# An FFN of selected tokens, computed for two batches at once by seven block products

## The chip, the cores and the metric

The kernel runs on one core of one Trainium2 chip. The metric is device time in microseconds of one execution; the median of three runs is given. The profile is one execution recorded by the hardware profiler; its span is a little shorter than the run's time.

Words for the engines: TensorE (PE) does matrix products, with PEld its loads of the stationary operand; VectorE (DVE) and ScalarE (ACT) do elementwise work and reductions, GpSimd (POOL) elementwise work in SBUF and gathers; SyncE (SP) issues transfers. PSUM is the memory that TensorE writes to.

## The reference

Attention with pooled queries feeds a mixture of depths: of each batch's 576 tokens the 128 with the highest gate score go through an FFN (512 to 1024 to 512 with a relu), the rest pass unchanged. Everything is fp32.

```
# q, k, v: (8 batches, 8 heads, 1152, 64); capacity 128
q_pool = q.reshape(B, H, S // 2, 2, D).mean(axis=3)
attn   = softmax(q_pool @ k.T / sqrt(D));  x = (attn @ v) as (B, 576, 512)
scores = einsum('bsd,d->bs', x, w_gate)
for b in range(B):
    top_idx = np.argpartition(-scores[b], capacity)[:capacity]
    xe = x[b, top_idx]                       # 128 x 512
    h  = np.maximum(xe @ w1, 0.0)            # w1: 512 x 1024
    ye = h @ w2                              # w2: 1024 x 512
    g  = 1.0 / (1.0 + np.exp(-scores[b, top_idx]))
    out[b, top_idx] = x[b, top_idx] + g[:, None] * ye
```

## The kernel before

The work is cut into 64 half-steps: 8 batches, 4 pairs of heads, 2 halves of the queries. In each, TensorE first makes the scores of this half, ScalarE takes their exponents, and TensorE then multiplies the exponents of the half before with the values.

```
        qs = slice(half["s"] * n, (half["s"] + 1) * n)
        p = half["p"] = self.work.tile([P, self.NG, G, 2, n], F32, name="p")
        for c in range(self.NC):
            sc = self.banks()
            for e in range(2):
                keys = slice(e * self.D, (e + 1) * self.D)
                for j in range(2):
                    rows = slice(j * self.D, (j + 1) * self.D)
                    nc.tensor.matmul(
                        sc[keys, j, 0:n],
                        lhsT=pair["kT"][rows, c * P + keys.start : c * P + keys.stop],
                        rhs=pair["qT"][rows, qs],
                        start=True,
                        stop=True,
                    )
            nc.scalar.activation(p[:, c // G, c % G, :, :], sc[:, :, 0:n], AF.Exp, scale=self.scale)

    # ... [cut] weighted(): the same loop with v, into one tile of two banks, then

        two = self.small.tile([P, 2, n], F32, name="two", bufs=2)
        nc.scalar.copy(two[:, :, :], av[:, :, 0:n])
        half["av"] = self.small.tile([P, n], F32, name="av", bufs=2)
        nc.gpsimd.tensor_tensor(
            out=half["av"][:, :], in0=two[:, 0, :], in1=two[:, 1, :], op=ALU.add
        )

    # ... [cut] folded(): the sums of exponents
        for u in range(G):
            nc.gpsimd.tensor_tensor(
                out=acc[:, u, :], in0=units[:, 0, u, :], in1=units[:, 1, u, :], op=ALU.add
            )
        fold = self.small.tile([P, 2, G * nb], F32, name="fold")
        for a, of in enumerate((units[:, 2, :, :], acc[:, :, :])):
            nc.vector.tensor_reduce(
                fold[:, a, :],
                of.rearrange("p u (m d) -> p (u m) d", d=BLK),
                AX.X,
                ALU.add,
                apply_transpose=True,
            )
```

For a pair to come, VectorE transposes keys and queries (`prepare_pair`: `kT`, L735, and `qT`) in even half-steps. Products with the gate weights and their sums:

```
        # multiplied():
        self.nc.gpsimd.tensor_tensor(
            out=pair["prod"][:, ns, :],
            in0=pair["avb"][:, ns, :],
            in1=self.w_gate[:, hp : hp + 1, :].broadcast_to([P, hb, BLK]),
            op=ALU.mult,
        )
        # ... [cut] gated():
        nc.vector.tensor_reduce(pair["red"][:, ns], pair["prod"][:, ns, :], AX.X, ALU.add)
        if half["s"] == 1:
            nc.vector.tensor_tensor(
                out=pair["part"][:, pair["hp"], :],
                in0=pair["red"][:, :],
                in1=pair["rec"][:, :],
                op=ALU.mult,
            )
```

A batch's tokens are ranked by VectorE (`routed`), their rows are gathered from the output in DRAM, transposed, put through both layers, added and scattered back. `yield` cuts this into pieces that the main loop takes between the attention products; a yield of `"mid"` or `"hidden"` says where. Here from the gather on:

```
            nc.gpsimd.indirect_dma_start(
                out=xe[0:w, :],
                out_offset=None,
                in_=rows_out,
                in_offset=bass.IndirectOffsetOnAxis(ap=index[0:w, 0:1], axis=0),
                bounds_check=(b + 1) * Sp - 1,
                oob_is_err=False,
            )

            xeT = ffn.tile([P, self.ND, P], F32, name="xeT")
            pv = self.banks()[:, 0, :].rearrange("p (c n) -> p c n", n=P)
            for c in range(self.ND):
                nc.tensor.transpose(
                    pv[:, c, 0:w], xe[0:w, c * P : (c + 1) * P], self.ident[0:w, 0:w]
                )
            nc.scalar.copy(xeT[:, :, 0:w], pv[:, 0 : self.ND, 0:w])
            yield mid

            hT = ffn.tile([P, self.NFC, P], F32, name="hT")
            for f0 in range(0, self.NFC, 4):
                pv = self.banks()[:, 0, :].rearrange("p (c n) -> p c n", n=P)
                for f in range(4):
                    for c in range(self.ND):
                        nc.tensor.matmul(
                            pv[:, f, 0:w],
                            lhsT=self.w1[:, c, (f0 + f) * P : (f0 + f + 1) * P],
                            rhs=xeT[:, c, 0:w],
                            start=(c == 0),
                            stop=(c == self.ND - 1),
                        )
                    if f == 3:
                        nc.scalar.activation(hT[:, f0 : f0 + 4, 0:w], pv[:, :, 0:w], AF.Relu)
                    yield "hidden" if f0 + f == self.NFC - 1 else False

            ps = self.banks()[:, 0, :]
            for f in range(self.NFC):
                nc.tensor.matmul(
                    ps[0:w, 0 : self.Dm],
                    lhsT=hT[:, f, 0:w],
                    rhs=self.w2[:, f, :],
                    start=(f == 0),
                    stop=(f == self.NFC - 1),
                )
                yield False
            if b == self.B - 1:
                nc.vector.scalar_tensor_tensor(
                    out=xe[0:w, :],
                    in0=ps[0:w, 0 : self.Dm],
                    scalar=own_gate[0:w, 0:1],
                    in1=xe[0:w, :],
                    op0=ALU.mult,
                    op1=ALU.add,
                )
            else:
                y = ffn.tile([P, self.Dm], F32, name="y", bufs=1)
                nc.scalar.activation(
                    y[0:w, :], ps[0:w, 0 : self.Dm], AF.Copy, scale=own_gate[0:w, 0:1]
                )
                if b < self.B - 2:
                    yield True
                nc.gpsimd.tensor_tensor(out=xe[0:w, :], in0=y[0:w, :], in1=xe[0:w, :], op=ALU.add)
            # ... [cut] scattered back by an indirect transfer
```

The main loop of half-steps, its body cut to the order of the work:

```
        for h in range(n_halves + 1):
            # ... [cut] even half-steps take the next pair; odd ones load another
                    pair["part"] = part
                else:
                    loaded = None
                    if n + 2 < len(pairs):
                        loaded = self.load_pair(*pairs[n + 2])
                        self.load_values(loaded)
                    if n > 1:
                        self.stored(halves[h - 4]["pair"])
                # ... [cut]
                self.scores(half)
                if h > 1:

                    of = halves[h - 2 - s]["pair"]
                    if s == 0:
                        of["groups"] = self.side_by_side(of["sum"].rearrange("p j n -> p (j n)"))
                    else:
                        self.spread(of)
                self.units(mid=True)
                if h > 2:
                    self.gated(halves[h - 3])
                self.folded(half)
                if h > 1:
                    self.multiplied(halves[h - 2])
                if s == 0 and loaded:
                    upcoming = loaded
                    self.prepare_pair(upcoming)
            # ... [cut] the last step, weighted(), drained(), normalized(), units(mid=False)
```

After the loop the remaining pieces of the last three batches are put in an order by hand: `older` (batch 5), `old` (batch 6), `new` (batch 7). Batch 7's scores are brought into a row by a matmul with a diagonal (L1054) and ranked from there.

```
        pieces(older, self.NFC - 2)
        pieces(new, 1)
        pieces(older, 2)
        pieces(new, 3)
        pieces(older)
        pieces(old, self.NFC)
        pieces(new, 1)
        low = self.counted()
        pieces(old, self.NFC - 3)
        pieces(new, 2)
        pieces(old)
        count = self.outside(low)
        pieces(new)
```

Of the kernel before, what the change touches and what calls it, by code (L numbers as in the profile page):

```python
# [534 lines left out]
class _Plain:  # L535
# [10 lines left out]
    def __init__(self, ctx, tc, q, k, v, moe_w_gate, moe_w1, moe_w2, capacity, out):  # L546
# [27 lines left out]
        assert 0 < self.TAIL < P and self.Dm == self.ND * P and self.Dm <= 512  # L574
        assert self.F == self.NFC * P and self.NFC % 4 == 0
# [17 lines left out]
        self.w2 = self.const.tile([P, self.NFC, self.Dm], F32, name="w2")  # L593

# [21 lines left out]
    def constants(self):  # L616
# [13 lines left out]
        slot_i = self.ffn.tile([P, self.Sp], I32, name="cmp", bufs=1)  # L630
        nc.gpsimd.iota(slot_i[:, :], pattern=[[1, self.Sp]], base=0, channel_multiplier=0)
        self.slot_f = const.tile([P, self.Sp], F32, name="slot_f")
        nc.vector.tensor_copy(self.slot_f[:, :], slot_i[:, :])
# [34 lines left out]
    def line_of_scores(self):  # L668

        line = self.ffn.tile([P, self.NT * P], F32, name="sc_row")  # L670
        self.nc.gpsimd.memset(line[0:1, self.Sp :], 0.0)
        return line
# [24 lines left out]

    def load_pair(self, b, hp):  # L700
# [3 lines left out]
        qb = self.load.tile([P, self.QB, 2, BLK], F32, name="qb")  # L704
# [8 lines left out]
    def load_values(self, pair):  # L713
# [3 lines left out]
        v_sb = pair["v"] = self.load.tile([P, 2, self.NC, self.D], F32, name="v_sb", bufs=3)  # L717
# [23 lines left out]
    def load_first(self, b, hp):  # L741
# [3 lines left out]
        kb = self.load.tile([P, self.KB, BLK], F32, name="kb")  # L745
        kn = kb.rearrange("p n d -> p (n d)").rearrange("p (c j d) -> p c j d", c=NC, j=2)
        acc = self.work.tile([P, G, 2 * self.HALF], F32, name="acc")
        third = self.QB // 3
        qn = acc.rearrange("p u n -> p (u n)")[0 : 3 * BLK, 0 : 4 * third * D]
        qn = qn.rearrange("p (j m d) -> p j m d", j=2, d=D)  # L750
        v_sb = self.load.tile([P, 2, NC, D], F32, name="v_sb", bufs=3)
# [11 lines left out]
        return {"k": kn, "q": qn, "v": v_sb, "b": b, "hp": hp}  # L763

    def prepare_first(self, pair):
# [5 lines left out]
        acc = self.work.tile([P, G, 2 * self.HALF], F32, name="acc")  # L771
        qp = acc.rearrange("p u n -> p (u n)")[0:rows, 0 : 2 * third * D]
        qp = qp.rearrange("p (n j d) -> p n j d", j=2, d=D)
# [76 lines left out]
    def folded(self, half):  # L850
# [9 lines left out]
        fold = self.small.tile([P, 2, G * nb], F32, name="fold")  # L860
# [8 lines left out]
        if half["s"] == 0:  # L869
            pair["sum"] = self.small.tile([P, 2, self.QB], F32, name="sum")  # L870
# [126 lines left out]
    def routed(self, b, part):  # L997
# [13 lines left out]
        if b < self.B - 1:  # L1011
# [27 lines left out]
            if b < self.B - 2:  # L1039
                yield True  # L1040
# [431 lines left out]
```

## Time and profile before

| | |
|---|---|
| median of 3 runs | 708.19 us (706.77 to 708.98) |
| span of the profiled execution | 704.8 us |
| matmuls of scores, L818 | 295.2 us busy |
| matmuls with the values, L836 | 294.6 us busy |
| first FFN layer, L1208 | 59.3 us busy, 512 instructions |
| second FFN layer, L1221 | 57.3 us busy, 128 instructions |
| bytes moved by transfers | 82.86 MB, 118 GB/s on average |

Lines named L... are lines of the kernel. A matmul in fp32 is recorded as two instructions. Busy times of matmuls overlap, so the sum over the lines is more than the time that they take. A row of the profile's table of groups gives line, engine, operation, operands, count, then the busy time, the mean duration in ns, and the idle time of the engine before them. The chain of work that ended last is followed back from the last instruction: at each step to what released it. A row of the waits gives who waited for what: total us, how often, the longest.

### The profile page before, as it was taken

The page shows a single profiled execution, that of the slowest core. Times are in us where ns is not written, and L with a number is a line of the kernel's source. Part 1 is how long each engine was busy: PE and PEld are TensorE (multiplying, and loading weights), DVE is VectorE, ACT ScalarE, POOL GpSimd, SP SyncE. Part 2 cuts the span into 40 slices and gives each one's busy share as a digit, 9 for nine tenths or more (in the row PEclk, how much of TensorE's full clock was granted, in tenths as well). Part 3 has the DMA queues.
Part 4 walks back from the last instruction along what each step waited for, and adds up shares of the span by engine and source line. Part 5 has one row for each costly group of instructions (what it writes and reads, how often), then busy time and mean ns, then how long its engine had stood idle before and what let it go on. Part 6 is the DMA issues. An engine that isn't in the chain of part 4 may idle for free.

```text
span 704.8 us, 23397 instructions
## 1 busy us (share of the span) xinstructions
PE 694.4 (99%) x9948; PEld 516.8 (73%) x9948; DVE 496.5 (70%) x793; ACT 444.5 (63%) x963; POOL 485.1 (69%) x452
## 2 busy tenths in 40 slices
PE   8999999999999999999999999999999999999996
PEld 5668899996758866688656887578775787766573
DVE  3877777996559965498754988559774697689540
ACT  6677778777547775477746776467754777477210
POOL 5877777868658695586955779467874877686520
PEclk9999999999999999999999999999999999999999
DMA  8888887858486483756928468382775728432200
GB/s 175 172 178 180 171 166 137 146 116 161 85 149 111 85 162 75 145 97 111 172 40 159 81 129 160 66 148 61 161 130 85 135 56 169 83 72 62 45 31 35
DMA packets 389490, 82.86 MB, mean 118 GB/s; under 512 B 376640, under 2 KB 376640, under 8 KB 389376
## 3 DMA queue, kind: packets, MB, share of 16 engines
q1 hardware_dynamic: 387872, 76.49, 58.1%
q0 software_dynamic: 1280, 4.20, 1.8%
q8 instruction: 80, 1.31, 0.8%
q10 hardware_dynamic: 224, 0.59, 0.3%
q14 instruction: 34, 0.28, 0.1%
HBM read 69.65 MB, written 11.59 MB: 115 GB/s over the span
## 4 chain that ended last, share of the span: by engine, by line
PE 89%; POOL 5%; issue 2%; DMA 1%; ACT 1%; DVE 1%; SPq 0%; POOLq 0%; DVEq 0%; ACTq 0%
PE ps L836 36%; PE ps L818 36%; PE ps L1208 8%; PE ps L1221 7%; POOL acc L857 2%; ACT p L825 1%; DMA kb<-in_k_dram 1%; DMA xe<-out_dram,index 1%; PE ps L1197 1%; POOL prod L925 1%; POOL x L956 0%; POOL av L846 0%; DVE fold L862 0%; POOL index L1175 0%; SPq L759 0%
## 5 line engine op out<-in xcount | busy, mean ns | idle before, releaser
L825 ACT ACTIVATE p<-ps 128x576 f32<-128x576 f32 x576 | 320.2, 695 | 1.7 <-PE ps L818 1.3
L818 PE MATMUL ps<-qT,kT 64*64 64x288 f32 x4608 | 295.2, 404 | 0.2 <-ACT p L825 0.2
L836 PE MATMUL ps<-p,v_sb 64*64 64x288 f32 x4608 | 294.6, 403 | 0.0
L857 POOL TENSOR_TENSOR acc<-p 128x576 f32<-128x576 f32 x192 | 266.3, 1417 | 15.4 <-ACT p L825 15.1
L836 PEld LDWEIGHTS ps<-p,v_sb 64*64 64x64 f32 x4608 | 215.5, 133 | 65.3 <-ACT p L825 9.2
L818 PEld LDWEIGHTS ps<-qT,kT 64*64 64x64 f32 x4608 | 208.0, 132 | 73.0 <-ACT p L825 15.4
L862 DVE TRANSPOSE_TENSOR_REDUCE fold<-p 128x54 f32<-128x1728 f32 x64 | 126.0, 1969 | 50.2 <-ACT p L825 50.2
L862 DVE TRANSPOSE_TENSOR_REDUCE fold<-acc 128x54 f32<-128x1728 f32 x64 | 125.3, 1957 | 46.0 <-POOL acc L857 45.8
L844 ACT COPY two<-ps 128x576 f32<-128x576 f32 x64 | 40.9, 639 | 156.9 <-PE ps L836 143.8
L846 POOL TENSOR_TENSOR av<-two 128x288 f32<-128x288 f32 x64 | 51.2, 800 | 96.5 <-ACT two L844 94.9
L915 DVE STREAM_TRANSPOSE avb<-av 128x288 f32<-128x288 f32 x64 | 29.4, 460 | 66.5 <-POOL av L846 66.5
L956 POOL TENSOR_TENSOR x<-avb,rec 128x576 f32<-128x576 f32 x32 | 37.1, 1159 | 40.3 <-DVE rec L954 27.9
L1208 PEld LDWEIGHTS ps<-xeT,w 128*128 128x128 f32 x512 | 57.8, 192 | 2.7 <-ACT p L825 2.6
L1208 PE MATMUL ps<-xeT,w 128*128 128x128 f32 x512 | 59.3, 277 | 0.0
L1221 PE MATMUL ps<-w,hT 128*128 128x512 f32 x128 | 57.3, 598 | 0.0
L925 POOL TENSOR_TENSOR prod<-avb,w_gate 128x288 f32<-128x288 f32 x64 | 51.5, 805 | 0.6 <-DVE avb L915 0.6
L902 ACT ACTIVATE sums<-total,tiny 32x18 f32<-32x18 f32 x124 | 38.1, 308 | 15.9 <-DVE total L893 14.2
L732 POOL TENSOR_TENSOR qp<-qb 128x576 f32<-128x576 f32 x31 | 43.8, 1414 | 2.2 <-DMA qb<-in_q_dram 2.2
L1221 PEld LDWEIGHTS ps<-w,hT 128*128 128x128 f32 x128 | 23.6, 190 | 28.1 <-issue 25.8
L735 DVE STREAM_TRANSPOSE kT<-kb 128x1152 f32<-128x1152 f32 x31 | 42.5, 1370 | 0.0
L887 ACT COPY groups<-sum 32x36 f32<-32x36 f32 x124 | 27.1, 219 | 6.7 <-DVE sum L872 5.2
L981 DVE TENSOR_TENSOR part<-red,rec 128x18 f32<-128x18 f32 x32 | 27.0, 845 | 1.1
(95 smaller groups left out, 290.6 us busy)
## 6 DMA issues: line engine op xcount, KB each, us to landing
kb<-in_k_dram SPq DMA_DIRECT2D x124, 144.0 KB
qb<-in_q_dram SPq DMA_DIRECT2D x124, 144.0 KB
v_sb<-in_v_dram SPq DMA_DIRECT2D x124, 144.0 KB
out_dram<-x SPq DMA_DIRECT2D x128, 72.0 KB
lines<-row_rank SPq DMA_DIRECT2D x7, 640.0 KB
w<-in_moe_w_dram SPq DMA_DIRECT2D x8, 512.0 KB
sc_row<-row SPq DMA_DIRECT2D x7, 288.0 KB
acc<-in_q_dram ACTq DMA_DIRECT2D x2, 288.0 KB
```

The costliest lines, as they stand in the source:

```text
L732: nc.gpsimd.tensor_tensor(out=qp[:, :, :], in0=pair["q"][:, :, 0, :], in1=pair["q"][:, :, 1, :], op=ALU.add)
L735: nc.vector.transpose(kT.rearrange("p (c g i) -> p c g i", c=self.NC, i=BLK), pair["k"].rearrange("p (g c) d -> p c g d", c=self.NC),)
L818: nc.tensor.matmul(sc[keys, j, 0:n], lhsT=pair["kT"][rows, c * P + keys.start : c * P + keys.stop], rhs=pair["qT"][rows, qs], start=True, ...
L825: nc.scalar.activation(p[:, c // G, c % G, :, :], sc[:, :, 0:n], AF.Exp, scale=self.scale)
L836: nc.tensor.matmul(av[j * self.D : (j + 1) * self.D, e, 0:n], lhsT=half["pair"]["v"][keys, j, c, :], rhs=half["p"][keys, c // G, c % G, j, :],
L844: nc.scalar.copy(two[:, :, :], av[:, :, 0:n])
L846: nc.gpsimd.tensor_tensor(out=half["av"][:, :], in0=two[:, 0, :], in1=two[:, 1, :], op=ALU.add)
L857: nc.gpsimd.tensor_tensor(out=acc[:, u, :], in0=units[:, 0, u, :], in1=units[:, 1, u, :], op=ALU.add)
L862: nc.vector.tensor_reduce(fold[:, a, :], of.rearrange("p u (m d) -> p (u m) d", d=BLK), AX.X, ALU.add, apply_transpose=True,)
L925: self.nc.gpsimd.tensor_tensor(out=pair["prod"][:, ns, :], in0=pair["avb"][:, ns, :], in1=self.w_gate[:, hp : hp + 1, :].broadcast_to([P, ...
L1208: nc.tensor.matmul(pv[:, f, 0:w], lhsT=self.w1[:, c, (f0 + f) * P : (f0 + f + 1) * P], rhs=xeT[:, c, 0:w], start=(c == 0), stop=(c == self ...
L1221: nc.tensor.matmul(ps[0:w, 0 : self.Dm], lhsT=hT[:, f, 0:w], rhs=self.w2[:, f, :], start=(f == 0), stop=(f == self.NFC - 1),)
```

## The change

For two batches the FFN's products are 2 x 2 block products: the tokens of two batches, each cut in two along the inner dimension, times the weights cut in quarters. Such a product needs eight block products done directly; with sums of the blocks taken beforehand seven are enough. The change does this for batches 0 to 5, in three pairs; batches 6 and 7 keep the direct layers. For it

- VectorE makes four sums of quarters of each layer's weights once, in sixteen pieces, one in each of the half-steps 11 to 26 (counted from 0); they are kept in DRAM and loaded back for each layer in turn into one tile `tw`;
- GpSimd makes four sums of the activations for each layer (`input_sums`);
- ScalarE copies each block product out of PSUM, and VectorE adds them in place (`seven_products`);
- ScalarE applies the relu to both batches' hidden values from SBUF, in one half-step; `scale` by the gate is then a step of its own.

To make room in SBUF several buffers are shared or fewer (query buffer 1 of 2, values 2 of 3, `prod` 1 of 2). The values are loaded one pair later. The product `part` goes from VectorE to GpSimd except at the end, `index` from GpSimd to VectorE, the division `x` to the following half-step. The order after the loop is new. TensorE's order of a pair is now: 56 matmuls of layer 1 in one half-step, three half-steps later 28 matmuls of layer 2; for the pair of batches 4 and 5 layer 2 stands after the last attention product.

```diff
+    def weight_sums(self):
+
+        nc = self.nc
+        for layer in (2, 1):
+            b11, b12, b21, b22 = (self.quarter(layer, i, j) for i in range(2) for j in range(2))
+            t1, t2, t3, t4 = (self.summed(layer, i) for i in range(4))
+            kept = self.tw_kept[layer] = self.dram.tile(
+                [P, 4, self.tw.shape[-1]], F32, name=f"tw{layer}", bufs=1
+            )
+            for i, (to, x, y) in enumerate(((t1, b12, b11), (t2, b22, t1), (t3, b22, b12), (t4, b21, t2))):
+                n = to.shape[1] // 2
+                for c in (slice(0, n), slice(n, 2 * n)):
+                    nc.vector.tensor_tensor(
+                        out=to[:, c, :], in0=x[:, c, :], in1=y[:, c, :], op=ALU.subtract
+                    )
+                    if c.start:
+                        nc.sync.dma_start(kept[:, i, :], self.tw[:, i, :])
+                    yield
+
+    def load_sums(self, layer):
+        for i in range(0, 4, 2):
+            self.nc.sync.dma_start(self.tw[:, i : i + 2, :], self.tw_kept[layer][:, i : i + 2, :])
+            yield
+
 
 
 # ... [cut] load_pair(): qb with bufs=1; load_values(): v_sb with bufs=2; multiplied(): prod with bufs=1
+            ending = pair["b"] == self.B - 1 and pair["hp"] >= self.NPAIR - 2
+            engine = nc.vector if ending else nc.gpsimd
+            engine.tensor_tensor(
                 out=pair["part"][:, pair["hp"], :],
                 in0=pair["red"][:, :],
                 in1=pair["rec"][:, :],
                 op=ALU.mult,
             )
 # ... [cut] routed(): after the transposes of the gathered rows
+            token = {"xe": xe, "xeT": xeT, "gate": own_gate, "index": index, "rows": rows_out, "w": w, "b": b}
+            if b >= self.paired:
+                yield mid
+                yield from self.layers(token)
+            elif b % 2 == 0:
+                self.first_of_two = token
 # ... [cut] else layers_of_two(); layers(): the two layers as before
+    def input_sums(self, a, s):
+
+        a11, a12, a21, a22 = a
+        s1, s2, s3, s4 = s
+        add, subtract = ALU.add, ALU.subtract
+        for i, (to, x, y, op) in enumerate(
+            ((s1, a21, a22, add), (s2, s1, a11, subtract), (s3, a11, a21, subtract), (s4, a12, s2, subtract))
+        ):
+            self.nc.gpsimd.tensor_tensor(out=to, in0=x, in1=y, op=op)
+            if i % 2:
+                yield i == 3
+
+    def seven_products(self, layer, a, s, c, rest, shape):
+
+
+
+        nc = self.nc
+        (a11, a12, _, a22), (s1, s2, s3, s4), (c11, c12, c21, c22) = a, s, c
+        b11, b21, b22 = (self.quarter(layer, i, j) for i, j in ((0, 0), (1, 0), (1, 1)))
+        t1, t2, t3, t4 = (self.summed(layer, i) for i in range(4))
+        u, x, y = rest
+
+        steps = (
+            (a11, b11, c11, ()),
+            (s1, t1, c22, ()),
+            (s3, t3, c21, ()),
+            (s2, t2, u, ((u, c11), (c21, u), (u, c22), (c22, c21))),
+            (s4, b22, c12, ((c12, u),)),
+            (a12, b21, x, ((c11, x),)),
+            (a22, t4, y, ((c21, y),)),
+        )
+        copies = []
+        for i, (of, by, to, _) in enumerate(steps):
+            if i % 2 == 0:
+                tile = self.banks()
+            ps, n = shape(tile[:, i % 2, :]), of.shape[1]
+            for f in range(by.shape[2] // P if layer == 1 else 1):
+                for k in range(n):
+                    if layer == 1:
+                        args = ps[:, f, :], by[:, k, f * P : (f + 1) * P], of[:, k, :]
+                    else:
+                        args = ps, of[:, k, :], by[:, k, :]
+                    nc.tensor.matmul(
+                        args[0], lhsT=args[1], rhs=args[2], start=k == 0, stop=k == n - 1
+                    )
+
+            copies.append((to, ps))
+            last = i == len(steps) - 1
+            if i % 2 or last:
+                for copy in copies:
+                    nc.scalar.copy(*copy)
+                copies = []
+            yield "sums" if last else False
+        for *_, sums in steps:
+            for to, of in sums:
+                nc.vector.tensor_tensor(out=to, in0=to, in1=of, op=ALU.add)
+
+    def layers_of_two(self, tokens):
+
+        nc, ffn, w = self.nc, self.ffn, tokens[0]["w"]
+
+        def quarters(tiles, n):
+            return [tile[:, i * n : (i + 1) * n, 0:w] for tile in tiles for i in range(2)]
+
+        def lines(bank):
+            return bank.rearrange("p (f n) -> p f n", n=P)[:, :, 0:w]
+
+        yield True
+        a = quarters([token["xeT"] for token in tokens], self.ND // 2)
+        room, s = self.room_of_sums(self.ND // 2, w)
+        for _ in self.input_sums(a, s):
+            pass
+        yield "mid"
+        hidden = [ffn.tile([P, self.NFC, P], F32, name="hT") for _ in tokens]
+        c = quarters(hidden, self.NFC // 2)
+
+        rest = [lines(room[:, i]) for i in (2, 3, 0)]
+        yield from self.seven_products(1, a, s, c, rest, lines)
+        yield "mid"
+        for tile in hidden:
+            nc.scalar.activation(tile[:, :, 0:w], tile[:, :, 0:w], AF.Relu)
+        loads = self.load_sums(2)
+        next(loads)
+        yield True
+        next(loads)
+        room, s = self.room_of_sums(self.NFC // 2, w)
+        for last in self.input_sums(c, s):
+            yield "hidden" if last else True
+
+        half = self.Dm // 2
+        third = hidden[1].rearrange("p f n -> p (f n)")
+        c11, c22, c21, c12 = third[:, 0:half], room[:, 0, half:], room[:, 2, 0:half], room[:, 2, half:]
+        rest = [room[0:w, i, 0:half] for i in (0, 3, 1)]
+        c = [of[0:w] for of in (c11, c12, c21, c22)]
+        yield from self.seven_products(2, quarters(hidden, self.NFC // 2), s, c, rest, lambda bank: bank[0:w, 0:half])
+        yield "mid"
+        for i, of in enumerate(c):
+            nc.scalar.activation(of, of, AF.Copy, scale=tokens[i // 2]["gate"][0:w, 0:1])
+        yield True
+        for i, of in enumerate(c):
+            token = tokens[i // 2]
+            to = token["xe"][0:w, i % 2 * half : (i % 2 + 1) * half]
+            nc.gpsimd.tensor_tensor(out=to, in0=of, in1=to, op=ALU.add)
+            if i % 2:
+                self.written(token)
+                yield True
+        if tokens[1]["b"] + 1 < self.paired:
+            for _ in self.load_sums(1):
+                yield True
 
 # ... [cut] run(): the half-step
+            if h > 10:
+                next(sums, None)
 # ... [cut]
+            self.units("mid")
+            if h > 2:
                 self.gated(halves[h - 3])
+            self.folded(half)
+            self.units("sums")
+            if h > 1:
                 self.multiplied(halves[h - 2])
 # ... [cut] run(): after the loop
+        self.gated(halves[-3])
+        self.weighted(halves[-1])
+        self.drained(halves[-1])
+        self.multiplied(halves[-2])
+        self.multiplied(halves[-1])
+        self.gated(halves[-2])
+        pieces(older, 1)
+        self.normalized(halves[-1]["pair"])
+        for half in (halves[-3], halves[-1]):
+            self.divided(half["pair"])
+            self.stored(half["pair"])
+        self.gated(halves[-1])
+        _, new, _ = self.routing.pop()
+
         pieces(new, 1)
         pieces(older, 2)
+        pieces(old, 1)
+        pieces(new, 1)
+        pieces(older, 1)
         pieces(new, 3)
-        pieces(older)
-        pieces(old, self.NFC)
+        pieces(older, 4)
+        pieces(old, self.NFC // 2 - 1)
         pieces(new, 1)
         low = self.counted()
-        pieces(old, self.NFC - 3)
+        pieces(old, self.NFC // 2 + 2)
+        pieces(older)
         pieces(new, 2)
         pieces(old)
```

## The prediction

> **What bounds the kernel now.** I read the engine row of the page first, then the chain of work that ended last, then that chain in order of time, then the waits, and last a table of busy time by stretches of two half-steps.
>
> The engine row of the page (busy us, share of the span, instructions):
>
> ```profile
> PE 694.4 (99%) x9948; PEld 516.8 (73%) x9948; DVE 496.5 (70%) x793; ACT 444.5 (63%) x963; POOL 485.1 (69%) x452
> ```
>
> TensorE is never free, and no other engine comes near it on average. A busy TensorE could still be one that is held up inside, so I looked at the pace in the chain by order of time (start us, duration us, what):
>
> ```profile
> 87.95 4.38 PE ps L836 x72
> ...
> 176.19 7.34 PE ps L1208 x64
> 183.53 4.53 PE ps L836 x72
> 192.42 7.06 PE ps L1221 x16
> 199.49 4.53 PE ps L836 x72
> ```
>
> The chain is TensorE nearly from end to end. One batch's first FFN layer (L1208) is 32 matmuls, recorded as 64 instructions, in 7.34 us: 7.34/64 = 114.7 ns each for 128 columns. Its second layer (L1221) is 8 matmuls, 16 records, in 7.06 us: 441 ns each for 512 columns. Two points give a line: (441 - 114.7)/384 = 0.85 ns per column and 5.9 ns fixed. So time goes with columns streamed, and the work per column is what the change lowers. The attention product that follows an FFN block takes 4.53 us instead of 4.38: each insertion costs some 0.15 us beside its own matmuls.
>
> The waits, those that I use:
>
> ```profile
> ACT two L844 <- PE ps L836: 143.8, 58, 4.0
> POOL av L846 <- ACT two L844: 94.9, 28, 7.3
> PEld ps L818 <- ACT p L825: 15.4, 58, 0.7
> ```
>
> The other engines wait for TensorE. ScalarE has 143.8/58 = 2.5 us of slack before the copy that ends a half-step; TensorE's own weight loads wait for ScalarE only 0.27 us a time, and the weight load runs ahead of the matmul, so most of that isn't lost.
>
> [...]
> - [...]The trace has two fp32 records per matmul[...]. A 256-column block has no row here; the line above gives 5.9 + 256 x 0.85 = 223.5 ns, an estimate.
> - [...]the diagonal product of L1044 took 759 ns.
> - [...]"part" (L981) has 18 elements, [...]and took 845 ns on average[...].
>
> **The change part by part.**
>
> *Layer 1 of a pair.* Two batches take 2 x 64 = 128 records now. The change does seven block products of 4 output tiles by 2 inner tiles, 56 matmuls or 112 records of 128 columns: 112 x 0.1147 = 12.85 us against 14.68. Saved 1.83 us.
>
> *Layer 2 of a pair.* Now 2 x 7.06 = 14.12 us. After: seven products of 4 matmuls with 256 columns, 56 records x 0.2235 = 12.52 us. Saved 1.60 us; one eighth would be 1.77, and the fixed part of the shorter matmul takes 0.17 back.
>
> Batches 0 to 5 are three pairs: 3 x (1.83 + 1.60) = 10.3 us. Batches 6 and 7 keep their old layers.
>
> *Insertions.* Twelve FFN blocks for these batches become six, so six seams of 0.15 us go: 0.9 us. (One of the twelve stands in the tail, where there may be no seam to save.)
>
> *Order at the end.* Batch 6's transposes (L1197) now stand between attention products and wait there for the gathered rows:
>
> ```profile
> 653.20 0.63 PE L1197 MATMUL ps<-ident,xe 128*128 128x128 f32 x4 [0.61 <-DMA xe<-out_dram,index]
> ```
>
> In the changed TensorE order they come after 12 matmuls of the pair's second layer. The 0.61 us should go. What fills the dead time of batch 7's routing there is now 12.5 us of pair layer 2 and 14.4 us of batch 6, instead of 7.06 + 14.4. From the last attention product to the diagonal matmul (L1054) took 6.0 us; its cover becomes 4 and 8 block matmuls (1.79 + 3.58), the row sums (0.25) and the transposes (0.61), 6.2 us. I expect this chain to stay covered.
>
> *VectorE.* Added: 16 sums of weights of 512 elements (0.69 us each, 11 us); per pair seven adds of 512 and seven of 256 elements (0.69 and 0.42 us), 23 us for three pairs[...]. Taken off: about 30 of the "part" products, 25 us, which go to GpSimd. Net +9 to +37 us, to 505 to 535 us in all. Where it is tightest is the stretch of batch 0's ranking (window, PE busy, PEld, VectorE, ScalarE, GpSimd, clock, DMA share, GB/s):
>
> ```profile
> 122.87:140.35 17.48, 17.48 (x293) 16.35 (x289) 15.43 (x26) 12.97 (x29) 14.15 (x14) 1.00 0.82 144
> 140.35:157.83 17.48, 17.48 (x293) 16.34 (x289) 16.27 (x35) 13.18 (x30) 12.93 (x13) 1.00 0.57 121
> ```
>
> VectorE is 31.7 of 35.0 us busy there. Four sums add 2.8 to 5.4 us, two "part" products take off 1.7: 32.8 to 35.4 us, full. But it needs to last only four half-steps: the key transposes of 137.98 are needed by TensorE some 5 us after their end, so a backlog of a microsecond or two should stay hidden.
>
> *ScalarE.* Per pair: seven copies out of PSUM of 512 (0.574 us, as L1200), two relus of 1024 from SBUF (about 1.0 us each, from L1200's 574 ns and L887's 219 ns for 36 elements), seven copies of 256 and four scalings (0.4 us each): 10.4 us against 3.7 now. The copies come while TensorE is in the block. The two relus fall in one ordinary half-step: 2.0 us into a slack of about 2.5, of which the routing's own ScalarE work sometimes takes 0.85. I allow 0.3 us of delay a pair, 0.9 us.
>
> *GpSimd.* Sums of activations of 256 and 512 elements (0.73 and 1.28 us by the line through L846's 800 ns for 288 and L857's 1417 ns for 576): 12 x 0.73 + 12 x 1.28 = 24 us; "part" 30 x 0.22 = 7 us; index (6.4 us) goes to VectorE. To about 510 us. The heaviest half-step has 8.3 us of usual work plus 2.5, over the 8.74 that TensorE needs; the next one holds a 12.5 us block, so it is paid back. Inputs come about 2 us before the product that reads them.
>
> *DMA.* 4 MB of sums stored and 10 MB loaded back, in long rows. The values of a pair are loaded one pair later and with one buffer less, and the query buffer is single: each still has about half a pair's time to spare. I expect no wait of TensorE.
>
> *Sum.* 10.3 + 0.9 + 0.6 = 11.8 us less on TensorE; 1.2 us of new waits (0.9 for the relus, 0.3 for the rest). 708.2 - 10.6 = 697.6; I say 697.5, 1.5% less.
>
> **The rivals.**
> 1. *Another engine becomes the bound.* VectorE's stretch above at 94 to 101%[...] could hold back the key transposes or the freeing of exponent buffers. For it: both tables above. Against it: the overload is short, and in steady stretches VectorE has 4 us free in 17.5. It would cost 3 to 8 us: 700 to 706, most of the gain.
> 2. *A wait for a transfer takes the place.* One load queue now also stores sums behind VectorE and waits for the single query buffer; a late load of keys or values would stop TensorE. For it: DMA share is 0.8 to 0.9 early on. Against it: that share falls to 0.57 by 157 us, and the blocks come later. Perhaps 2 to 5 us: 700 to 703.
> 3. *The block products run at the pace of the weight load*, not of the columns, or ScalarE's copies hold back the PSUM banks[...].
> 4. *A little more than the count.* No new wait at all and the tail a bit shorter: 695.5 to 696.5.
>
> **Range and chances.** TensorE's count is firm to about 1 us. What can go wrong is almost all to the slow side, though four of five times I expect under 4 us of it: 695.3 to 702. Faster by over 2% needs less than 694.0, beyond what the removed matmuls give: 0.06. Slower by over 2% needs 722, a stall of 25 us: 0.03. Within 2%: 0.91.
>
> **What would show each step right or wrong.** TensorE must stay at 98 to 99% busy, with a pair's first block at 12.85 us and its second at 12.5 us in the chain. If the second is above 13, rival 3 holds. If TensorE shows idle time before the score matmuls (after the key transposes or exponents), rival 1; before weighted products or released by a DMA, rival 2. The half-step with the relus should be at most 0.5 us longer than 8.74. The wait of 0.61 us for the gathered rows should be gone. A half-step above 8.74 us over many steps, outside the blocks, would make the prediction wrong.

## The result, and the profile after

The changed kernel takes 712.2 us (median of 4 runs, 709.52 to 712.81) beside 707.5 us for the kernel before (median of 4 runs, 706.57 to 708.98). The ratio is 1.0059, with an interval of 1.0035 to 1.0084. It is slower by 0.6%. The prediction was 697.5 us with a range up to 702.0, so both its size and its direction are wrong.

The profile's span went from 704.8 to 710.7 us. The engine row after:

```profile
PE 686.6 (97%) x9972; PEld 522.0 (73%) x9972; DVE 516.2 (73%) x827; ACT 462.8 (65%) x1005; POOL 515.2 (72%) x504
```

TensorE's busy time fell by 7.8 us (694.4 to 686.6). Its free time rose by 13.7 us, from 704.8 - 694.4 = 10.4 to 710.7 - 686.6 = 24.1. So the matmuls did get fewer, and more than that was lost in waiting. VectorE, ScalarE and GpSimd are each as busy as the prediction said (505 to 535; 444.5 + 3 x (10.4 - 3.7) = 465; 510), and none is near full.

The matmuls themselves, by TensorE's order of time (start us, duration us, what). First the pair of batches 0 and 1:

```profile
266.58 2.05 PE L1365 MATMUL ps<-xeT,w 128*128 128x128 f32 x16
...
279.28 4.59 PE L870 MATMUL ps<-p,v_sb 64*64 64x288 f32 x72
...
305.68 1.99 PE L1365 MATMUL ps<-w,hT 128*128 128x256 f32 x8
...
317.96 2.41 PE L870 MATMUL ps<-p,v_sb 64*64 64x288 f32 x36
```

Layer 1 of the pair goes from 266.58 to 279.28: 12.70 us (predicted 12.85). Layer 2 goes from 305.68 to 317.96: 12.28 us (predicted 12.52). These blocks are right, a little shorter than predicted.

What TensorE waited for, in the waits after (engine, line, what it waited for: us in total, times, longest):

```profile
PE ps L852 <- ACT two L878: 7.6, 7, 2.5
PE ps L1058 <- DVE line L1044: 2.4, 1, 2.4
PE ps L852 <- DVE qT L773: 2.1, 3, 0.8
PE ps L1090 <- DVE rank_parts L1112: 1.8, 1, 1.8
PE ps L817 <- DMA p<-in_k_dram: 1.5, 2, 1.0
PE ps L616 <- POOL ones L609: 1.0, 1, 1.0
PE ps L1189 <- DVE pick L1180: 0.7, 1, 0.7
```

The two of 1.5 and 1.0 us are the start and stood before too. The others are new or longer; the largest is scores (L852) held back because ScalarE had not yet copied out (`two`, L878) the PSUM banks that they are to use. Why was ScalarE late? The waits of the other engines, two rows of the kernel before and then the kernel after:

```profile
DVE fold L862 <- POOL acc L857: 45.8, 26, 3.6
ACT sums L902 <- DVE total L893: 14.2, 7, 2.8
```

```profile
DVE fold L896 <- POOL acc L891: 79.0, 40, 5.1
POOL part L1020 <- DVE red L1015: 61.6, 21, 6.4
...
ACT sums L936 <- DVE total L927: 21.9, 11, 3.6
```

ScalarE waits for VectorE's sums of exponents (21.9 us, before 14.2), VectorE for GpSimd's (`acc`; 79.0 us, before 45.8), and GpSimd, ahead of `acc`, for `red`, which is VectorE's again; in the kernel before `part` was VectorE's and there was no such wait on GpSimd. The group of `part` shows how little work hangs on that:

```profile
L1020 POOL TENSOR_TENSOR part<-red,rec 128x18 f32<-128x18 f32 x30 | 6.8, 226 | 72.5 <-DVE red L1015 61.6
```

It works for 6.8 us, and GpSimd stands idle in front of it for 72.5 us. One turn of the loop, in GpSimd's timeline (idle time before an instruction and its releaser in brackets):

```profile
148.12 0.24 POOL L1155 TENSOR_SCALAR gate<-gate 128x5 f32<-128x5 f32 x1
154.72 0.23 POOL L1020 TENSOR_TENSOR part<-red,rec 128x18 f32<-128x18 f32 x1 [6.36 <-DVE red L1015]
154.90 4.15 POOL L891 TENSOR_TENSOR acc<-p 128x576 f32<-128x576 f32 x3
```

VectorE in the same stretch:

```profile
153.59 0.68 DVE L720 TENSOR_TENSOR tw<-w 128x512 f32<-128x512 f32 x1
154.19 0.44 DVE L1015 TENSOR_REDUCE red<-prod 128x9 f32<-128x288 f32 x1
154.55 1.97 DVE L896 TRANSPOSE_TENSOR_REDUCE fold<-p 128x54 f32<-128x1728 f32 x1
159.08 1.98 DVE L896 TRANSPOSE_TENSOR_REDUCE fold<-acc 128x54 f32<-128x1728 f32 x1 [2.56 <-POOL acc L891]
...
161.35 0.38 DVE L927 TENSOR_REDUCE total<-groups 32x36 f32<-32x144 f32 x1
```

ScalarE, and then TensorE:

```profile
161.77 1.27 ACT L936 ACTIVATE sums<-total,tiny 32x18 f32<-32x18 f32 x4 [2.51 <-DVE total L927]
163.06 0.64 ACT L878 COPY two<-ps 128x576 f32<-128x576 f32 x1
```

```profile
157.73 4.64 PE L870 MATMUL ps<-p,v_sb 64*64 64x288 f32 x72
163.83 4.60 PE L852 MATMUL ps<-qT,kT 64*64 64x288 f32 x72 [1.45 <-ACT two L878]
```

GpSimd is free at 148.36 and stands until `red` ends at 154.6. Then it makes three sums that it might have begun earlier. VectorE, now itself without work for 2.56 us, takes the last sum at 159.08; each following step is late by the chain of order, and at the end TensorE stands for 1.45 us. The same is seen around 241 us (2.54 us) and, by way of `line`, at 595 us (2.43 us).

A gap can cost more than its length. The table of stretches around the gap that ends at 595.51 us (stretch, its length, busy us and count of TensorE, PEld, VectorE, ScalarE, GpSimd; then TensorE's granted clock as a share of full speed, DMA share, GB/s):

```profile
594.00:597.00 3.00, 1.49 (x10) 1.19 (x10) 2.97 (x6) 1.61 (x6) 3.00 (x5) 0.73 0.22 36
597.00:602.00 5.00, 5.00 (x69) 2.85 (x72) 4.25 (x5) 0.65 (x2) 4.66 (x4) 0.82 1.00 193
602.00:606.00 4.00, 4.00 (x72) 2.30 (x66) 2.19 (x5) 3.43 (x7) 2.64 (x4) 1.00 0.63 106
```

The clocks of 0.73 and 0.82 are averages. Cut finer, the granted clock is 0.50 from 595.4 to 598.8 us and 1.00 on both sides of that. TensorE's next product of 72 takes 5.48 us instead of 4.6. It isn't so behind every gap. The longest of this run left the clock at 1.00, and the product behind it took its usual time:

```profile
241.73 4.60 PE L852 MATMUL ps<-qT,kT 64*64 64x288 f32 x72 [2.54 <-ACT two L878]
```

### The profile page after: what moved, and what is told of

The parts are those of the page before. It is cut to its first block, busy times and chain, and to the rows that moved or that the text cites. A ratio compares the mean times of both kernels' runs of the same rounds, so it can differ in the third digit from the quotient of the medians.

```text
span 710.7 us, 23604 instructions
## 1 busy us (share of the span) xinstructions
PE 686.6 (97%) x9972; PEld 522.0 (73%) x9972; DVE 516.2 (73%) x827; ACT 462.8 (65%) x1005; POOL 515.2 (72%) x504
## 5 line engine op out<-in xcount | busy, mean ns | idle before, releaser
L852 PE MATMUL ps<-qT,kT 64*64 64x288 f32 x4608 | 294.9, 404 | 9.7 <-ACT two L878 7.6
L891 POOL TENSOR_TENSOR acc<-p 128x576 f32<-128x576 f32 x192 | 273.1, 1451 | 7.1 <-ACT p L859 7.1
L852 PEld LDWEIGHTS ps<-qT,kT 64*64 64x64 f32 x4608 | 204.7, 132 | 87.8 <-ACT p L859 13.2
L878 ACT COPY two<-ps 128x576 f32<-128x576 f32 x64 | 40.7, 636 | 109.0 <-PE ps L870 106.4
L1020 POOL TENSOR_TENSOR part<-red,rec 128x18 f32<-128x18 f32 x30 | 6.8, 226 | 72.5 <-DVE red L1015 61.6
L936 ACT ACTIVATE sums<-total,tiny 32x18 f32<-32x18 f32 x124 | 38.2, 308 | 23.6 <-DVE total L927 21.9
L1015 DVE TENSOR_REDUCE red<-prod 128x9 f32<-128x288 f32 x64 | 27.3, 426 | 0.4 <-POOL prod L959 0.4
L1128 DVE TENSOR_SCALAR_CACHE_REDUCE pick<-sc_row,gate_sc 128x576 f32<-128x576 f32 (+4 forms) x40 | 21.6, 540 | 4.0 <-ACT gate_sc L682 3.7
L1373 ACT COPY s<-ps 128x256 f32<-128x256 f32 (+1 forms) x27 | 11.4, 447 | 19.6 <-PE ps L1365 19.6
L906 DVE TENSOR_REDUCE sum<-fold 128x18 f32<-128x108 f32 x64 | 21.8, 341 | 2.2
```

The costliest lines, as they stand in the source:

```text
L852: nc.tensor.matmul(sc[keys, j, 0:n], lhsT=pair["kT"][rows, c * P + keys.start : c * P + keys.stop], rhs=pair["qT"][rows, qs], start=True, ...
L891: nc.gpsimd.tensor_tensor(out=acc[:, u, :], in0=units[:, 0, u, :], in1=units[:, 1, u, :], op=ALU.add)
L936: self.nc.scalar.activation(tot[rows, :], pair["total"][:, j * self.QB : (j + 1) * self.QB], AF.Identity, bias=self.tiny[0:BLK, 0:1],)
```

## The experiments

Theory 1, *order*: GpSimd works in order, and `part` on it stands ahead of the sums of exponents and waits for VectorE's `red`; what VectorE has ahead of `red` reaches TensorE through this. Theory 2, *load*: VectorE has simply too much to do, above all by the weight sums, and would hold TensorE back with any order. Each time is beside the kernel before on the same chip (706.7 to 707.5 us).

### `part` back on VectorE

```diff
-            engine = nc.vector if ending else nc.gpsimd
+            engine = nc.vector
```

> The one edit: the product part of all pairs is made by VectorE again, where it stood before the change. Theory 1 (GpSimd waits in its order for VectorE's late sum red before it may begin the exponent sums, and this closes a loop GpSimd, VectorE, ScalarE, TensorE): TensorE's waits for the copy two (7.6 us) and for qT (2.1 us) fall to 2 us or less in all, the wait of part (72.5 us) is gone from GpSimd, and the time is 701 to 704 us. Theory 2 (VectorE has simply too much work since the sums of weights came): VectorE gets 30 times some 0.8 us more, the waits stay or grow, 712 to 715 us.

Measured: 697.0 us (692.36 to 700.97), ratio 0.9828 [0.9775, 0.9882]. The changed kernel's loss turns into a gain by one word. VectorE has more to do than in the changed kernel (553.4 us busy, held-up time included), so load as such isn't the cause. The time is lower than the expected 701 to 704 us. The four times are two near 693 and two near 701; more of this below.

### `part` on GpSimd, behind the sums of exponents

```diff
-            engine = nc.vector if ending else nc.gpsimd
-            engine.tensor_tensor(
 # ... [cut] the rest of the product, which moves into a function parted()
+            if ending:
+                self.parted(pair, nc.vector)
 # ... [cut] run():
             self.folded(half)
+            if h > 3 and s == 0:
+                old_pair = halves[h - 3]["pair"]
+                if not (old_pair["b"] == self.B - 1 and old_pair["hp"] >= self.NPAIR - 2):
+                    self.parted(old_pair, nc.gpsimd)
             self.units("sums")
```

> The one edit: part stays on GpSimd, but behind the three exponent sums of its half-step instead of ahead of them; no work is added or taken away on any engine. Theory 1 (the place in GpSimd's order): as good as with part on VectorE or better, 700 to 703 us, TensorE waits for two below 1 us. Theory 2 (too much work for VectorE): nothing changes, 711 to 713 us.

Measured: **692.8 us** (691.71 to 693.87), ratio 0.9786 [0.977, 0.9802]: faster than both kernels, and by more than expected (700 to 703). No work is taken off any engine; one product of 0.22 us a pair changes its place. The engine row, and all that TensorE still waits for:

```profile
PE 682.3 (99%) x9972; PEld 529.7 (77%) x9972; DVE 526.8 (76%) x827; ACT 462.6 (67%) x1005; POOL 515.0 (74%) x504
```

```profile
PE ps L817 <- DMA p<-in_k_dram: 1.1, 2, 0.6
PE ps L616 <- POOL ones L609: 1.0, 1, 1.0
PE ps L1193 <- DVE pick L1184: 0.7, 1, 0.7
PE ps L1094 <- DVE rank_parts L1116: 0.4, 1, 0.4
```

The same stretch of GpSimd's timeline as above:

```profile
147.91 4.16 POOL L891 TENSOR_TENSOR acc<-p 128x576 f32<-128x576 f32 x3 [0.77 <-ACT p L859]
153.51 0.22 POOL L1028 TENSOR_TENSOR part<-red,rec 128x18 f32<-128x18 f32 x1 [1.44 <-DVE red L1015]
```

The three sums begin at 147.9 instead of 154.9, 0.77 us after GpSimd is free, and `part` waits 1.44 us, with that urgent work already done.

### Without the weight sums, with either place of `part`

Both kernels leave the sixteen subtractions of weights out: `tw` holds a constant and the FFN's values are not the reference's. Transfers and all other instructions stay. The first has `part` where the change put it, the second behind the sums of exponents.

```diff
-                    nc.vector.tensor_tensor(
-                        out=to[:, c, :], in0=x[:, c, :], in1=y[:, c, :], op=ALU.subtract
-                    )
```

> Leaves out the sixteen subtractions of weights on VectorE (the tile tw is set to a constant once, so the values of batches 0 to 5 are not the reference's); stores, loads and all else as in the change. Theory 2: the waits of TensorE between 160 and 265 us are gone, 8 us or more come back, 702 to 704 us, with GpSimd's wait ahead of part still there. Theory 1: the sums only push red back by 0.7 to 1.8 us in half-steps that would wait anyway, so that half of those waits remain: 706 to 709 us.

> The kernel with part behind the exponent sums, and without the sixteen subtractions of weights (tw is set to a constant, so the values of batches 0 to 5 are not the reference's). The order theory: with the order right VectorE's 15 us for the sums stand beside other work, and leaving them out brings nothing: 691.5 to 693.5 us. The work theory: another 3 to 6 us come back, 687 to 690.

Measured: 698.5 us (697.33 to 704.52), ratio 0.9889 [0.9836, 0.9942], for the first. To take 15.4 us of work off VectorE (8.3 and 7.1 us in the two groups of L720) brings 712.2 - 698.5 = 13.7 us back, more than either theory expected and nearer to the load theory; to move `part` brought 19.4. But of TensorE's waits two stay, in half-steps that have no weight sum:

```profile
PE ps L1057 <- DVE line L1043: 2.4, 1, 2.4
PE ps L1089 <- DVE rank_parts L1111: 1.8, 1, 1.8
```

and `part` still waits 57.1 us for `red`. The second takes 694.2 us (692.58 to 696.25), ratio 0.9812 [0.9788, 0.9837]: no faster than with the subtractions (692.8). So the weight sums cost nothing once the order is right. The place of `part` in the change costs about 4 us without the sums (698.5 - 694.2) and 19.4 us with them (712.2 - 692.8): work ahead of `red` makes that place costly, and the same load alone does nothing.

### Two other ways to bring `red` forward

In the first, the piece of weight sums moves from the head of the half-step to behind `red`. In the second, `red` and `part` move to the end of the half-step before, ahead of its last pieces of ranking; `part` still stands ahead of `acc` on GpSimd.

```diff
 # first
-            if h > 10:
-                next(sums, None)
 # ... [cut]
                 self.gated(halves[h - 3])
+            if h > 10:
+                next(sums, None)
 # second
-            if h > 2:
-                self.gated(halves[h - 3])
 # ... [cut] the end of the half-step
+            if h > 1:
+                self.gated(halves[h - 2])
 # ... [cut] after the loop the first self.gated(halves[-3]) goes
```

> The change with one edit: in VectorE's order the piece of the sums of weights comes behind red and ahead of the exponents' reductions, instead of ahead of both. No work is added or taken away. The order theory: GpSimd gets red earlier by one subtraction, 0.7 to 1.8 us, so that part of the waits go, mostly those for two between 160 and 265 us: 703 to 708 us. The work theory: 711 to 713.

> The change with one edit: red and part (gated) are placed at the end of the half-step before, ahead of the ranking pieces in VectorE's order; on GpSimd part stays ahead of the exponent sums. No work is added or taken away. The order theory: GpSimd's wait ahead of part shrinks from 2.4 us each to about 1, TensorE's waits are gone, and the time is near that with part behind the exponent sums: 692 to 697 us. The work theory: 709 to 713.

Measured: 708.3 us (706.99 to 712.15, 20 runs), ratio 1.0009 [0.9996, 1.0022], and 701.6 us (700.33 to 702.61), ratio 0.9918 [0.9901, 0.9934]. Both go the way that order says, since no work is taken away, but the first lies just above the range expected, and the second gains 10.6 us where 15 to 20 were expected. The waits say why: `part` still waits 55.8 and 47.4 us for `red`. VectorE's folds and transposes also stand ahead of `red` (in the second kernel `red` begins at 150.95 us, behind two folds that begin at 146.30 and 148.19), so to shift single pieces gives only a part.

### The same move in the kernel before

```diff
-            nc.vector.tensor_tensor(
+            ending = pair["b"] == self.B - 1 and pair["hp"] >= self.NPAIR - 2
+            engine = nc.vector if ending else nc.gpsimd
+            engine.tensor_tensor(
```

> The kernel before with one edit: part (but for the last two pairs) on GpSimd, ahead of the exponent sums, as the change has it. Theory 1: GpSimd waits for red here too, 4 to 6 us in each ranking half-step; TensorE begins to wait for two, the time rises by 1 to 4 us to 708.5 to 712. Theory 2: VectorE is relieved of 27 us, the time is the same or a little less, 706 to 708.

Measured: 729.5 us, ratio 1.0313 [1.0296, 1.0331]. Slower, far more than expected, and at another end. TensorE's largest wait:

```profile
PE ps L1199 <- DMA xe<-out_dram,index: 14.5, 6, 3.3
```

In this kernel the transposes of the gathered rows have little spare time, and the gather is later (issued at 164.82 us where the kernel before has 161.19). The order on GpSimd is at work here too. With `part` ahead of it the first of the exponent sums begins at 133.67 us instead of 131.09, and at 153.59 instead of 149.97; VectorE, which also ranks, waits for these sums in order (74.6 us in all, in the kernel before 45.8), and the ranking and the gather get later with it. `line`, which reads `part`, adds 1.1 us a time. Six waits of up to 3.3 us follow. The granted clock is 0.50 for 3.4 us at two of them (from 170.5 and from 675.6 us), where the products of 72 took 6.06 and 6.28 us; TensorE's busy time grew from 694.4 to 700.9 us. The expectation had the sign and the order, but neither the size nor the place: `part` itself waits only 13.4 us here, and what TensorE waits for is the gathered rows and not `two` (1.8 us).

### Direct layers, with `part` behind the sums

```diff
-        self.paired = self.B - 2 - self.B % 2
+        self.paired = 0
```

> The kernel with part behind the exponent sums (692.8 us), but with no batch paired: all eight batches by the two direct layers, no sums of weights or activations; all the rest of the change stays. If the 10.3 us of matmuls that the prediction counted for the block products are real time once nothing waits, this takes them back and half a microsecond to one of seams: 703 to 705 us. If the gain over the kernel before comes from the new order of the rest (values loaded later, division later, batch 6 at the end), this stays at 693 to 697.

Measured: 713.4 us (711.75 to 713.78), ratio 1.0075 [1.0058, 1.0092], 20.6 us more than the same kernel with block products; expected were 10 to 12. TensorE's busy time differs by 696.3 - 682.3 = 14.0 us and its free time by 15.1 - 9.8 = 5.3 us. The first is the 10.3 us of matmuls and 3.7 us more. Of these the blocks, measured shorter than predicted, are 1.2 (3 x (14.68 - 12.70 + 14.12 - 12.28) = 11.5 us saved), and perhaps 1.3 are clock (in the tail it is 0.50 for 6.8 us here and for 3.4 us there; layer 1 of all batches is busy for 62.2 us here and for 59.3 in the kernel before; layer 1 of batches 6 and 7 for 16.6 us there and for 15.0 in the same kernel without weight sums). The rest stays open. The second are waits in the tail (L1094 2.7 us, L1193 2.3 us), whose order was made for the block products. So this kernel is no clean measure of the block products alone.

### `part` on VectorE: two groups of times

The four times of `part` on VectorE asked for a cause. Its profile, of a run of 701.0 us, holds this in VectorE's timeline:

```profile
407.71 9.82 DVE L1020 TENSOR_TENSOR part<-red,rec 128x18 f32<-128x18 f32 x1
417.46 1.97 DVE L896 TRANSPOSE_TENSOR_REDUCE fold<-p 128x54 f32<-128x1728 f32 x1
```

A product of 18 elements per partition, whose median is 0.43 us, takes 9.82 us. GpSimd meanwhile:

```profile
405.28 4.13 POOL L891 TENSOR_TENSOR acc<-p 128x576 f32<-128x576 f32 x3
409.38 0.79 POOL L959 TENSOR_TENSOR prod<-avb,w_gate 128x288 f32<-128x288 f32 x1
410.14 1.40 POOL L766 TENSOR_TENSOR qp<-qb 128x576 f32<-128x576 f32 x1
411.51 0.79 POOL L880 TENSOR_TENSOR av<-two 128x288 f32<-128x288 f32 x1
412.26 1.15 POOL L993 TENSOR_TENSOR x<-avb,rec 128x576 f32<-128x576 f32 x1
413.38 4.12 POOL L891 TENSOR_TENSOR acc<-p 128x576 f32<-128x576 f32 x3
424.50 0.80 POOL L959 TENSOR_TENSOR prod<-avb,w_gate 128x288 f32<-128x288 f32 x1 [7.01 <-DVE avb L949]
```

GpSimd runs without a gap until 417.50, and VectorE's product ends at 417.53. The same kernel was profiled twice more, unchanged.

> The same kernel as the one with part back on VectorE, looked at again, because its four times fell into two groups (692.4 and 693.8; 700.2 and 701.0 us) and the profiled one, 701.0, holds two part products of 9.82 and 6.30 us among 32 with a median of 0.43 us, each begun while GpSimd ran a chain of products without a gap. Theory (a VectorE product with two operands in SBUF is kept waiting not for one GpSimd instruction but until GpSimd pauses, and this is what parts the two groups): in a profile with a time near 693 us no part is longer than 2 us; near 700 us at least one is longer than 5 us, and TensorE has a wait of 2 us or more behind it. Rival (the groups come from something else, such as transfers or the clock): long part products in a profile near 693, or none in one near 700.

> As the look before it, for a second profile of the same kernel: near 693 us with no part longer than 2 us, or near 700 us with at least one longer than 5 us, by the theory of the wait for GpSimd's pause; the rival expects no such tie between the two.

Measured: 693.4 us with one `part` of 6.28 us and no new wait of TensorE above 0.7 us; 700.4 us with one of 4.42 us and one of 10.40 us, and a wait of 5.7 us (L852 for `two`). As worded, the expectation failed in the first: a hold-up of 6 us stays hidden there. What goes with 700 us in both such profiles is one of about 10 us, with a wait of TensorE of 4.7 or 5.7 us behind it. That ties the longer time to the long hold-up in three profiles; what makes one execution have it and the next not is not shown.

The last kernel has `part` in the place of the 692.8 us kernel, but on VectorE:

```diff
-                    self.parted(old_pair, nc.gpsimd)
+                    self.parted(old_pair, nc.vector)
```

> part on VectorE, but after its two folds of the half-step, where GpSimd has ended the exponent sums and is about to run out of work. If the wait for GpSimd's pause parts the two groups of the kernel with part on VectorE, it should be rarer and shorter here: no part above 3 us, all times 692 to 695 us, one group. The rival expects two groups again, 693 and 700 us, median 693 to 700. [...]

Measured: 706.0 us (703.93 to 708.49, 12 runs), ratio 0.9988 [0.9974, 1.0002]. Both guesses missed: the hold-up is not rarer behind the folds. Two of `part` take 5.79 and 5.78 us, and here the transposes of keys and queries stand right behind them, so both reach TensorE:

```profile
353.15 7.47 PE L852 MATMUL ps<-qT,kT 64*64 64x288 f32 x72 [4.37 <-DVE qT L773]
528.60 6.79 PE L852 MATMUL ps<-qT,kT 64*64 64x288 f32 x72 [5.68 <-DVE qT L773]
```

The 72 scores after these gaps take 7.47 and 6.79 us instead of 4.6. So 10.0 us of waiting and some 5 us of slower clock (0.50 for 6.8 us at each gap) make up the 14.5 us between the spans of this kernel (706.6 us) and of the one with `part` on GpSimd in the same place (692.1 us).

## Why the prediction was wrong

- *Layers of a pair, insertions, the gathered rows:* right. The blocks took 12.70 and 12.28 us where 12.85 and 12.52 were predicted, and the wait of 0.61 us is gone. With the order mended, TensorE's busy time is 694.4 - 682.3 = 12.1 us lower than before, where the count had 10.3 + 0.9 = 11.2, and the span 704.8 - 692.1 = 12.7 us shorter, where it had 11.8. By the medians it is 14.7 us faster (707.5 and 692.8); the shorter blocks explain 1.2 us of the difference to the count, the rest isn't explained.
- *VectorE, ScalarE, DMA:* the sums of busy time were right (VectorE 516.2 us in 505 to 535). The adds took 688 ns and 422 ns as said (a line through the products of 384 and 576 elements in the kernel before, 554 and 759 ns, gives 691 and 417), the relus delay no half-step, no transfer stops TensorE after the start. The weight sums took 893 to 1038 ns on average, inside what was allowed (5.4 us for four, the author's estimate): the eight with no GpSimd product beside them 0.63 to 0.69 us, the eight beside one 0.81 to 1.82 us, and each of these ended 0.55 us after a GpSimd product did. But 28 us in the upper end of +37, 42 x 0.67 us, were the author's estimate of hold-ups by GpSimd for the adds. None came: the adds ran with no GpSimd product beside them. The sixteen weight sums had nothing of it in the sum and took 15.4 us instead of 11.
- *GpSimd, the term "part 30 x 0.22 = 7 us":* **this is the step that failed.** The work was 6.8 us, but the term counts only work. GpSimd takes its instructions in order; `part` stands ahead of the sums of exponents and needs `red`, behind pieces of ranking and weight sums on VectorE. GpSimd stood idle for 72.5 us ahead of it, and to place it behind the sums of exponents takes 19.4 us off the kernel's time.
- *The sum's "1.2 us of new waits", and rival 1's "the overload is short":* wrong through it. TensorE's free time grew by 13.7 us where the sum has 1.2 - 0.6 = 0.6. TensorE's busy time is also 686.6 - 682.3 = 4.3 us more than with the order mended. Some 1.5 us of this are slower clock behind the gap at 595 us, where three products took 0.58, 1.09 and 5.48 us; behind the same wait in the first kernel without sums they took 0.37, 0.63 and 4.59. The rest is probably not slower work: matmuls overlap (a product of 72 is recorded with 4.64 us, and without a gap the next begins 4.37 us after it), and ahead of a gap the end of the last one counts as busy. The scores at 163.83 us begin 6.10 us after the product before them, with the order mended 4.37; that is 1.73 us late, of which the idle time shows 1.45. Together: predicted -11.2 + 0.6 = -10.6, measured in the profile -7.8 + 13.7 = +5.9.
- *Rival 1* named VectorE and said 700 to 706. Its mechanism, an overload of VectorE, isn't the cause by itself: VectorE is busier with `part` behind the sums (526.8 us) than in the changed kernel (516.2), and TensorE waits less. What VectorE does ahead of `red` counts only through the order. Rivals 2 and 3 did not occur. *Rival 4*, nothing lost beside the count, is what the mended kernel does; with 692.8 us it lies below that rival's 695.5 to 696.5 and below the whole range.

That the place of `part` is the cause is shown, by the kernel that changes only that and gains 19.4 us. How the 5.9 + 10.6 = 16.5 us between prediction and profile divide between single gaps and clock is read from one profile. Why the direct layers cost 20.6 us and not 11 beside it stays partly open.

## What to carry to other kernels

When a small instruction moves to another engine, don't cost it by its duration: ask what it waits for, what stands behind it in that engine's order, and who waits for those. Look in the groups at the idle time ahead of an instruction, not at its busy time; put an instruction with a late input behind the engine's urgent work. Busy shares of 65 to 79% told nothing here of either danger, the wait in order on GpSimd or the hold-up on VectorE.

## What the runs showed of the hardware

A VectorE product with two operands in SBUF can be held up by far more than one GpSimd instruction. In the kernel before, all 32 `part` products took 0.62 to 0.92 us, and each ended 0.03 to 0.04 us after a GpSimd product beside it; in 31 of the 32 GpSimd went on with its next without a pause. With `part` back on VectorE the shortest took 0.18 us. With it there or behind the folds, the runs show 4.4 to 10.4 us in seven products of four profiles, where a GpSimd product of the chain printed above takes 0.8 to 1.4 us; and all seven ended within 0.05 us of the end of a GpSimd instruction. In the case printed above this was the last of a chain of ten. Five of the seven ended as GpSimd stopped for 0.16 us or more; in the other two (6.30 and 4.42 us) GpSimd went on at once or after 0.11 us, so a long pause isn't needed. Nor is it so every time: of the 32 such products of the profile above most took 0.2 to 0.9 us, some of them beside a running chain. What decides it no run here shows.

The granted clock can fall at a short gap. In these traces the clock is either 1.00 or 0.50, and inside a run it stayed at 0.50 for 3.4 or 6.8 us. It fell at each of the five gaps of 3.3 us or more; the products after those of 4.37 and 5.68 us took 2.9 and 2.2 us longer. Shorter gaps aren't safe, and their length doesn't decide: of twelve gaps from 1.9 to 2.7 us, those at the start left aside, four had it and eight had not. In the changed kernel it fell at 2.43 us and not at 2.54, and in the first kernel without weight sums the same wait of 2.43 us left it at 1.00. It also fell behind a gap of only 0.69 us, at 677.3 us in the changed kernel, and with the order mended behind one of 0.70 us, at 657.9. What decides it is not shown.
